# Another list schedule for a chunked attention, and a last row tile finished block by block

## The chip, the cores and the metric

The kernel runs on one core of one Trainium2 chip. The metric is the device time of one execution in microseconds. Every time below that carries a start is counted from the start of the profiled execution's span.

## What is computed

A linear attention with a complex decay feeds a mixture of eight experts, of which each token takes one, and this feeds a plain two-layer network.

```python
B, H, S, D = 4, 8, 768, 48
# attention: per batch and head, over t
S_re, S_im = ar * S_re - ai * S_im + k[t] (x) v[t], ar * S_im + ai * S_re
y[t] = q[t] @ S_re
# experts: x is y as 3072 tokens x 384
e = argmax(x @ w_gate)
x = softmax(x @ w_gate)[e] * sigmoid(x @ w_output_gate)[e] * (relu(x @ w1[e]) @ w2[e])
# second network: 384 -> 2048 -> 384
h = x @ w_in
out = maximum(0.01 * h, h) @ w_out
```

## The kernel before

The sequence is cut into six chunks of 128 positions (`c` from 0 to 5); the four batches form two groups of two (`g`). For each chunk and group an elementwise chain on ScalarE and VectorE makes, from the decay `a`, its logarithm `l` and angle `th`; TensorE sums both over the positions by a product with a triangle (`cum`, 384 columns of moving data, lines 525 and 539); then sine, cosine and the exponentials `ep` and `em` scale q and k into the tiles `qk` (lines 558 and 559).

For each batch and each half of its eight heads there is then a step (`b_step`), 48 in all, with these blocks on TensorE:

- two times four transposes of `qk` into the PSUM tile `tp` (line 603), each copied to `qT` or `kT` by ScalarE or VectorE;
- the scores `sc` (line 612), which VectorE masks into `sT` (line 615);
- the product `yp` of `sT` with v, and from chunk 1 on of `qT` with the state `Z` (lines 624 and 628);
- the state product `kv` (line 639), which VectorE adds to `Z`;
- after the second half four transposes of the result `yT` into `tp` (line 650), copied to `xo`.

After each chunk TensorE makes the logits of the gate (line 583; `lgm`), VectorE routes the tokens (`route`), and POOL scatters the rows `xo` to slots of their expert in `xs_d`. After the last chunk `ranks` orders the experts by size, which the expert layers' loads need.

A TensorE block uses 128, 64 or 32 columns of the array: the rows of the trace write 128\*128, 128\*64 and 128\*32. Transposes, scores and sums use 128, `yp` and `kv` use 64, the gate's logits 32. PSUM tiles rotate: three buffers for `cum`, two for `tp`, one for `sc`.

The order of all this isn't written out by hand. Each piece is recorded as an operation with an engine, a duration in microseconds, the tiles it reads and writes and a priority (`Schedule.op`); `plan` then takes, again and again, the operation that can start first, the one of lower priority number on a tie, and `emit` writes the instructions in that order. Each engine runs its instructions in this order. Priorities are a chunk's base plus an entry of the table `PRIO`.

What follows is written in program order: the expert layers (lines 960 to 962 are the three products of a split into a high and a low part: `hp` the first layer, then the second), and the second network over six row tiles of 512 tokens, `i` from 0 to 5, with 16 slices `f` of its hidden layer each. For a slice TensorE makes nine products into `hp`; ScalarE and VectorE make from it `g`, `gh` and `gl` (lines 1193, 1194, 865 and 868). `second` then multiplies `gh` and `gl` by the slice's weights for four blocks of 128 tokens and adds into the PSUM tiles `yq0` to `yq3`, three matmuls a block. It runs one slice late: the list `late` holds the slice before. After slice 15 each `yq` is scaled into `ot` by ScalarE or VectorE (lines 1177 and 1175) and POOL scatters its rows to the output (line 1178).

Of the kernel before, what the change touches and what calls it, by code (L numbers as in the profile page):

```python
# [20 lines left out]
B, H, S, D = 4, 8, 768, 48  # L21
# [19 lines left out]
NW = NTOK // TW  # L41
# [6 lines left out]

PRIO = {"trig": -14.28, "exp": -4.36, "scaled": 2.94, "next": -3.57, "second": -29.47, "turn": 0.75, "state": 2.81, "rows": 1.73, "gate": -0.63, "route": 12.2}
CUM_BUFS, TP_BUFS, SC_BUFS = 3, 2, 1  # L50
# [48 lines left out]
class Schedule:  # L99
# [14 lines left out]

    def op(self, eng, dur, fn, reads, writes, prio, epoch=None, lat=0.0, gate=None):
        i = len(self.ops)
        deps = set()
        for b in reads:
            deps.update(b.writers)
        for b in writes:  # L120
            deps.update(b.readers)
            deps.update(b.writers)
        new = []
        for b in list(reads) + list(writes):
            r = b.root
            if r.first is None and r.tile is None:
                r.first = i
                new.append(r)
            if i not in r.users:
                r.users.append(i)  # L130
        for b in writes:
            b.writers, b.readers = [i], []
        for b in reads:
            if b not in writes:
                b.readers.append(i)
        deps.discard(i)
        if isinstance(eng, str):
            eng, dur = (eng,), {eng: dur}
        self.ops.append(dict(i=i, uses=[b.root for b in list(reads) + list(writes)], engs=eng, dur=dur, fn=fn, deps=deps, prio=(prio, i), epoch=epoch, new=new, lat=lat, gate=gate))

    def plan(self, table_of, switch=1.28):
# [5 lines left out]
        left = {e: sum(1 for o in ops if o["epoch"] == e) for e in epochs}  # L147
        rings, cur = {}, None

# [3 lines left out]
        def ready(o, eng):  # L153
            t = free.get(eng, 0.0)
            for d in o["deps"]:
                if d not in end:
                    return None
                t = max(t, end[d] + self.LAT.get(by[d], 0.16) + (0.1 if eng == "pe" and by[d] != "pe" else 0.0))
# [7 lines left out]
            for b in o["new"]:  # L166
                ring = rings.setdefault(b.tag, [])
                if len(ring) >= b.bufs:
                    for u in ring[-b.bufs].users:
                        if u not in end:  # L170
                            return None
                        t = max(t, end[u] + 0.2)
            return t

        while todo:
# [13 lines left out]
            i = o["i"]  # L189
            by[i] = eng  # L190
            free[eng] = t + o["dur"][eng]
            end[i] = t + o["dur"][eng] + o["lat"]
            if o["epoch"] is not None:
# [167 lines left out]
def tile_kernel(ctx: ExitStack, tc: tile.TileContext, q, k, v, a_re, a_im, wg, w1, w2, w_in, w_out, cbig, csmall, seq, vseq, wgn, out):  # L361
# [202 lines left out]
    def logits(c, bs, pr):  # L564
# [15 lines left out]
        def lgm():  # L580
            for p2 in range(4):
                for i, b in enumerate(bs):
                    nc.tensor.matmul(out=lp.t[i * 32:(i + 1) * 32], lhsT=WG[:, p2], rhs=yTt[c, b].t[:, p2], start=(p2 == 0), stop=(p2 == 3))
        S.op(PE, 1.2, lgm, [yTt[c, b] for b in bs], [lp], pr)
        ls = S.buf(rt, [P, P], F32, "ls", 2)
# [5 lines left out]
    def b_step(c, b, hh, pr):  # L591
# [28 lines left out]
        def av():  # L620
            for p2 in range(2):
# [3 lines left out]
                if c > 0:  # L625
                    for i in range(2):
                        h = p2 * 2 + i
                        nc.tensor.matmul(out=yp.t[i * 64:i * 64 + 64, hh * 2 + p2], lhsT=Z[:, b, hh * 4 + h], rhs=qT.t[:, h], start=False, stop=True)  # L628
        S.op(PE, 0.51 if c == 0 else 1.04, av, [vt, sT, qT, Zb[b]], [yp], pr)
        if c < NCH - 1:  # L630
# [5 lines left out]
            def kvm():  # L636
                for h in range(4):
                    for i in range(2):
                        nc.tensor.matmul(out=kv.t[i * 64:i * 64 + 64, hh * 4 + h], lhsT=src.t[:, h0 + h, i], rhs=vt.t[:, h0 + h, :D], start=True, stop=True)  # L639
            S.op(PE, 0.61, kvm, [src, vt], [kv], pr + PRIO["state"])  # L640
            if hh == 1:
# [542 lines left out]
    for i in range(NW):  # L1184
        xh, xl = xhl.pop(("b", i))
        for f in range(NF):
# [8 lines left out]
            split(g, hh, hl)  # L1195
            if late:
                second(*late.pop(), range(TT))
# [12 lines left out]
            if f in (9, 11, 13) and i + 1 < NW:  # L1210
                t_split(i + 1, ((f - 9) // 2,))
    second(*late.pop(), range(TT))
    assert done[1] == len(jobs)
# [41 lines left out]
```

## Time and profile before

| what | value |
|---|---|
| median of three runs | 917.2 us (916.55 to 917.49) |
| the profiled execution, its own time | 916.85 us |
| its span in the trace | 915.1 us |
| TensorE busy, share of the span | 881.8 us, 96% |
| VectorE busy | 561.6 us, 61% |
| ScalarE busy | 465.0 us, 51% |
| load of `xe` (672 KB), issue to landing, median | 6.0 us |

The span is what the trace covers; the execution's own time is 1.75 us longer. A TensorE row's busy time runs from the start of its first matmul to the modelled end of its last, and the next block starts before that end; so how long a block takes is read from its start to the start of the next block.

### The profile page before, as it was taken

Reading aid. Unit: us, or ns where it says so; the run is one execution under the profiler, and the core shown is the slowest. Engines: PE = TensorE matmul, PEld = TensorE weight load, DVE = VectorE, ACT = ScalarE, POOL = GpSimd, SP = SyncE. Lnnn points to the kernel's source line nnn. Section 1 sums busy time; section 2 is a strip of 40 time slices with the busy share of each in tenths; the row PEclk is TensorE's granted clock in tenths of the full one; section 3 lists DMA queues with packets and bytes.
Section 4 is the critical chain, followed back from the end, with each engine's and each line's share of the span. In section 5 each row is a group of like instructions: output and inputs, shape, how many; then the busy total and the mean of one; then the engine's idle time right before and its main releaser. Section 6 shows DMA issues by size and latency. Waiting matters only on the chain.

```text
span 915.1 us, 14879 instructions
## 1 busy us (share of the span) xinstructions
PE 881.8 (96%) x5941; PEld 782.0 (85%) x5941; DVE 561.6 (61%) x970; ACT 465.0 (51%) x765; POOL 97.8 (11%) x90
## 2 busy tenths in 40 slices
PE   7888999999979999999999999999999999999996
PEld 3667878887869999999999889999998989899995
DVE  4678999897965767787756533454454454454332
ACT  6898887877633444455555433333343333333232
POOL 5000202101211830000000000100100101001001
PEclk8998999999989999999999999999999999999999
DMA  9834475212345998898867103004004004000001
GB/s 324 355 93 144 163 283 160 81 62 93 131 126 179 207 243 288 272 310 265 271 214 235 43 0 138 36 1 138 36 1 138 35 1 151 22 1 18 19 1 37
DMA packets 56092, 121.58 MB, mean 133 GB/s; under 512 B 8432, under 2 KB 24480, under 8 KB 56016
## 3 DMA queue, kind: packets, MB, share of 16 engines
q1 hardware_dynamic: 49792, 100.87, 34.3%
q0 software_dynamic: 6224, 19.69, 5.8%
q8 instruction: 48, 0.79, 0.4%
q14 instruction: 28, 0.23, 0.1%
HBM read 89.46 MB, written 31.08 MB: 132 GB/s over the span
## 4 chain that ended last, share of the span: by engine, by line
PE 78%; issue 9%; DVE 8%; ACT 3%; DMA 1%; POOL 0%; SPq 0%; POOLq 0%; DVEq 0%; ACTq 0%
PE hp L961 9%; PE hp L960 9%; PE hp L962 9%; PE yq L962 6%; PE yq L960 6%; PE yq L961 6%; PE sc L612 5%; PE tp L603 5%; PE yp L960 3%; PE yp L962 3%; PE yp L961 3%; PE yp L624 3%; PE kv L639 2%; PE cum L525 2%; PE yp L628 2%
## 5 line engine op out<-in xcount | busy, mean ns | idle before, releaser
L960 PE MATMUL hp<-xh,wh 128*128 128x512 f32 (+8 forms) x504 | 186.2, 370 | 1.2 <-DVE hl L1042 1.0
L962 PE MATMUL hp<-xh,wl 128*128 128x512 f32 (+8 forms) x504 | 186.5, 370 | 0.0
L961 PE MATMUL hp<-xl,wh 128*128 128x512 f32 (+8 forms) x504 | 186.4, 370 | 0.1
L1194 DVE TENSOR_TENSOR g<-g,hp 128x512 f32<-128x512 f32 x96 | 65.9, 687 | 156.3 <-ACT g L1193 154.8
L1193 ACT ACTIVATE g<-hp 128x512 f32<-128x512 f32 x96 | 57.4, 597 | 185.2 <-PE hp L962 185.2
L960 PE MATMUL yq<-wh,gh 128*128 128x384 f32 x384 | 129.7, 338 | 0.8 <-ACT gh L865 0.8
L962 PE MATMUL yq<-wh,gl 128*128 128x384 f32 x384 | 129.7, 338 | 0.2
L961 PE MATMUL yq<-wl,gh 128*128 128x384 f32 x384 | 129.0, 336 | 0.0
L868 DVE TENSOR_TENSOR gl<-g,gh 128x512 fp32r<-128x512 f32 x96 | 66.5, 692 | 67.1 <-PE yq L962 39.8
L960 PEld LDWEIGHTS hp<-xh,wh 128*128 128x128 f32 x504 | 95.8, 190 | 12.6 <-DVE hl L1042 3.4
L962 PEld LDWEIGHTS hp<-xh,wl 128*128 128x128 f32 x504 | 95.6, 190 | 12.7
L961 PEld LDWEIGHTS hp<-xl,wh 128*128 128x128 f32 x504 | 95.6, 190 | 9.7 <-DVE xl L868 0.2
L865 ACT ACTIVATE gh<-g 128x512 fp32r<-128x512 f32 x96 | 60.7, 632 | 73.5 <-DVE g L1194 73.5
L1178 POOL DMA_INDIRECT out<-ot,gpair x24 | 24.2, 1009 | 557.7 <-ACT ot L1177 551.8
L868 DVE TENSOR_TENSOR wl<-raw,wh 128x1536 fp32r<-128x1536 f32 x40 | 70.2, 1754 | 20.0 <-ACT wh L865 20.0
L960 PEld LDWEIGHTS yq<-wh,gh 128*128 128x128 f32 x384 | 72.2, 188 | 5.9 <-ACT gh L865 1.6
L961 PEld LDWEIGHTS yq<-wl,gh 128*128 128x128 f32 x384 | 72.3, 188 | 4.3
L962 PEld LDWEIGHTS yq<-wh,gl 128*128 128x128 f32 x384 | 72.0, 188 | 0.9 <-DVE gl L868 0.9
L960 PE MATMUL yp<-hh,wh 128*128 128x448 f32 (+6 forms) x192 | 68.3, 356 | 0.0
L962 PE MATMUL yp<-hh,wl 128*128 128x448 f32 (+6 forms) x192 | 67.1, 350 | 0.0
L961 PE MATMUL yp<-hl,wh 128*128 128x448 f32 (+6 forms) x192 | 67.1, 350 | 0.0
L603 PE MATMUL tp<-CB,qk 128*128 128x128 f32 x384 | 57.5, 289 | 8.3 <-DVE qk L559 4.8
(165 smaller groups left out, 1421.5 us busy)
## 6 DMA issues: line engine op xcount, KB each, us to landing
raw<-w SPq DMA_DIRECT2D x32, 768.0 KB, 6.3
vt<-v SPq DMA_DIRECT2D x12, 512.0 KB, 4.5
raw<-w_in SPq DMA_DIRECT2D x8, 768.0 KB, 8.6
wf<-w SPq DMA_DIRECT2D x16, 384.0 KB, 3.4
raw<-w_out SPq DMA_DIRECT2D x8, 768.0 KB, 6.0
raw<-wf SPq DMA_DIRECT2D x8, 768.0 KB, 5.6
xs_d<-zero POOLq DMA_DIRECT2D x4, 1344.0 KB, 16.4
xe<-xs_d SPq DMA_DIRECT2D x7, 672.0 KB, 6.0
```

Source lines behind the costliest of these rows:

```text
L525: S.op(PE, 0.64, lambda fp=fp, a=a, z=z: nc.tensor.matmul(out=fp.t, lhsT=TRI[c % 2], rhs=th.ap(a, z), start=True, stop=True), [cbb] + th.b ...
L603: nc.tensor.transpose(tp.t[:, h, :], src.t[:, h0 + h].rearrange("p a d -> p (a d)"), IDN)
L612: nc.tensor.matmul(out=sc.t[:, h, :], lhsT=kT.t[:, h], rhs=qT.t[:, h], start=True, stop=True)
L624: nc.tensor.matmul(out=yp.t[i * 64:i * 64 + 64, hh * 2 + p2], lhsT=vt.t[:, h0 + h], rhs=sT.t[:, h], start=True, stop=(c == 0))
L865: nc.scalar.activation(out=hi, in_=src, func=AF.Copy)
L868: nc.vector.tensor_tensor(out=lo, in0=src, in1=hi, op=ALU.subtract)
L960: nc.tensor.matmul(out=out, lhsT=ah, rhs=bh, start=first, stop=False)
L961: nc.tensor.matmul(out=out, lhsT=ah, rhs=bl, start=False, stop=False)
L962: nc.tensor.matmul(out=out, lhsT=al, rhs=bh, start=False, stop=last)
L1178: put = nc.gpsimd.indirect_dma_start(out=rows, out_offset=bass.IndirectOffsetOnAxis(ap=gpair.bitcast(I32)[:, j, 0:1], axis=0), in_=ot, in_ ...
L1193: nc.scalar.activation(out=g, in_=hp, func=AF.Copy, scale=0.01)
L1194: nc.vector.tensor_tensor(out=g, in0=g, in1=hp, op=ALU.max)
```

## The change

The planner is told how many columns of the array an operation uses (`cols`: 128 unless given), and adds 0.1 us (`TURN`) to the start of a TensorE operation whose columns differ from those of the one before. The durations of the narrow operations are set anew, and so is the table of priorities. In the last row tile slices 12 to 15 of the hidden layer are no longer multiplied as they come: `late` keeps them, and after slice 15 the second layer goes block by block, for each block over the four slices.

```diff
-PRIO = {"trig": -14.28, "exp": -4.36, "scaled": 2.94, "next": -3.57, "second": -29.47, "turn": 0.75, "state": 2.81, "rows": 1.73, "gate": -0.63, "route": 12.2}
+PRIO = {"trig": -14.49, "exp": -4.24, "scaled": 2.34, "next": -1.95, "second": -47.41, "turn": -1.83, "state": 19.8, "rows": 2.33, "gate": -35.61, "route": 10.98}
...
+    TURN = 0.1
+
+    def op(self, eng, dur, fn, reads, writes, prio, epoch=None, lat=0.0, gate=None, cols=128):
...
-        rings, cur = {}, None
+        rings, cur, array = {}, None, 128
...
             t = free.get(eng, 0.0)
+            if eng == "pe" and o["cols"] != array:
+                t += self.TURN
...
             free[eng] = t + o["dur"][eng]
+            if eng == "pe":
+                array = o["cols"]
...
-        S.op(PE, 1.2, lgm, [yTt[c, b] for b in bs], [lp], pr)
+        S.op(PE, 1.2, lgm, [yTt[c, b] for b in bs], [lp], pr, cols=32)
...
-        S.op(PE, 0.51 if c == 0 else 1.04, av, [vt, sT, qT, Zb[b]], [yp], pr)
+        S.op(PE, 0.45 if c == 0 else 0.9, av, [vt, sT, qT, Zb[b]], [yp], pr, cols=64)
...
-            S.op(PE, 0.61, kvm, [src, vt], [kv], pr + PRIO["state"])
+            S.op(PE, 0.5, kvm, [src, vt], [kv], pr + PRIO["state"], cols=64)
...
-            if late:
+            if late and not (i == NW - 1 and f > NF - 4):
                 second(*late.pop(), range(TT))
             late.append((i, f, hh, hl))
...
-    second(*late.pop(), range(TT))
+
+    for t in range(TT):
+        for x in late:
+            second(*x, (t,))
```

Each engine keeps its instructions but for about a dozen copies out of PSUM that change between ScalarE and VectorE; what moves is the order. Line numbers of the changed kernel are 6 to 9 higher. Three places show it. The first is TensorE from the logits of chunk 1 on, where the first batches of chunk 2 are worked on. Before:

```order
L583 MATMUL cum<-yT,WG 32x128 x16
L624 MATMUL yp<-sT,vt 64x128 x2
L628 MATMUL yp<-qT,Z 64x128 x2
L624 MATMUL yp<-sT,vt 64x128 x2
L628 MATMUL yp<-qT,Z 64x128 x2
L650 MATMUL tp<-CB,yT 128x128 x4
L612 MATMUL sc<-qT,kT 128x128 x4
L639 MATMUL kv<-vt,qk_108 64x48 x8
L603 MATMUL tp<-CB,qk_107 128x128 x4
L603 MATMUL tp<-CB,qk_108 128x128 x4
L588 MATMUL cum<-CB,ls 128x128
L639 MATMUL kv<-vt,qk_108 64x48 x8
```

And in the changed kernel, from the same logits:

```order
L589 MATMUL cum<-yT,WG 32x128 x16
L630 MATMUL yp<-sT,vt 64x128 x2
L634 MATMUL yp<-qT,Z 64x128 x2
L630 MATMUL yp<-sT,vt 64x128 x2
L634 MATMUL yp<-qT,Z 64x128 x2
L645 MATMUL kv<-vt,qk_108 64x48 x8
L630 MATMUL yp<-sT,vt 64x128 x2
L634 MATMUL yp<-qT,Z 64x128 x2
L630 MATMUL yp<-sT,vt 64x128 x2
L634 MATMUL yp<-qT,Z 64x128 x2
L645 MATMUL kv<-vt,qk_108 64x48 x8
L594 MATMUL cum<-CB,ls 128x128
```

Here the first dimension of the output is the number of columns used. The products `yp` and `kv` of two steps now stand together, and the score block and the transposes that stood among them have moved ahead of the logits or behind the group.

The second place is ScalarE where chunk 1's exponentials are made, just behind its seventh table load; `s` are tiles of the logarithms of chunk 2. Before:

```order
L457 ACTIVATE s_759<-ar 128x768
L541 ACTIVATE ep<-cum 128x384
L457 ACTIVATE s_779<-s_759 128x768
L471 ACTIVATE yT<-yp 128x512
L541 ACTIVATE em<-cum 128x384
L457 ACTIVATE s_795<-ar 128x768
L457 ACTIVATE s_779<-th 128x768
L457 ACTIVATE s_808<-s_795 128x768
L457 ACTIVATE s_779<-s_779 128x768
L471 ACTIVATE xo<-tp 128x384
L471 ACTIVATE qT<-tp 128x512
```

And in the changed kernel:

```order
L463 ACTIVATE s_784<-ar 128x768
L547 ACTIVATE ep<-cum 128x384
L463 ACTIVATE s_791<-s_784 128x768
L547 ACTIVATE em<-cum 128x384
L463 ACTIVATE s_799<-ar 128x768
L463 ACTIVATE s_805<-s_799 128x768
L463 ACTIVATE s_791<-th 128x768
L477 ACTIVATE qT<-tp 128x512
```

The copies `yT` and `xo` of chunk 0 no longer stand ahead of chunk 1's first `qT`; they have moved to the other side of the table load, and one elementwise instruction has moved behind `qT`.

The third place is the end of TensorE's work, the last matmuls into `yq` (with the tiles' numbers: `gh_9079` is slice 15 before). Before:

```order
L960 MATMUL yq2_8670<-wh_6164,gh_9079 128x384
L961 MATMUL yq2_8670<-wl_6165,gh_9079 128x384
L962 MATMUL yq2_8670<-wh_6164,gl_9080 128x384
L960 MATMUL yq3_8674<-wh_6164,gh_9079 128x384
L961 MATMUL yq3_8674<-wl_6165,gh_9079 128x384
L962 MATMUL yq3_8674<-wh_6164,gl_9080 128x384
```

And in the changed kernel, where `gh_8992` to `gh_9055` are slices 12 to 15:

```order
L966 MATMUL yq3_8674<-wh_6164,gh_8992 128x384
L967 MATMUL yq3_8674<-wl_6165,gh_8992 128x384
L968 MATMUL yq3_8674<-wh_6164,gl_8993 128x384
L966 MATMUL yq3_8674<-wh_6164,gh_9021 128x384
L967 MATMUL yq3_8674<-wl_6165,gh_9021 128x384
L968 MATMUL yq3_8674<-wh_6164,gl_9022 128x384
L966 MATMUL yq3_8674<-wh_6164,gh_9038 128x384
L967 MATMUL yq3_8674<-wl_6165,gh_9038 128x384
L968 MATMUL yq3_8674<-wh_6164,gl_9039 128x384
L966 MATMUL yq3_8674<-wh_6164,gh_9055 128x384
L967 MATMUL yq3_8674<-wl_6165,gh_9055 128x384
L968 MATMUL yq3_8674<-wh_6164,gl_9056 128x384
```

The last twelve matmuls all belong to the last block, where before each block had three of them; in return the first-layer products of slice 14 stand 12 matmuls earlier and those of slice 15 stand 24 earlier.

## Rows read from the trace of the kernel before

**Rows 1.** Busy time by engine in stretches; then granted clock, DMA share, GB/s.

```profile
core 0: us, PE busy (x) PEld busy (x) DVE busy (x) ACT busy (x) POOL busy (x), PEclk, DMA share, GB/s
...
30.28:78.74 48.46, 40.99 (x375) 31.47 (x376) 39.41 (x68) 43.54 (x72) 0.00 (x0) 0.93 0.52 184
78.74:84.00 5.26, 5.26 (x49) 4.91 (x52) 3.52 (x6) 3.49 (x7) 0.00 (x0) 0.70 0.58 220
84.00:254.80 170.80, 169.84 (x2022) 140.77 (x2014) 156.27 (x352) 133.44 (x228) 25.57 (x23) 1.00 0.39 134
...
268.64:907.34 638.70, 635.68 (x3336) 588.02 (x3336) 336.56 (x457) 258.19 (x407) 51.61 (x45) 1.00 0.37 118
907.34:915.10 7.76, 0.00 (x0) 0.00 (x0) 0.62 (x1) 0.09 (x1) 3.21 (x4) 0.76 0.31 108
```

**Rows 2.** TensorE's waits, 84 to 254.8: total, times, longest.

```profile
PE sc L612 <- ACT kT L471: 0.6, 1, 0.6
```

**Rows 3.** Timeline of TensorE: start, busy, line, operation, count.

```profile
70.99 0.62 PE L639 MATMUL kv<-vt,qk 128*64 128x48 f32 x16
...
82.71 1.16 PE L612 MATMUL sc<-qT,kT 128*128 128x128 f32 x8
83.80 1.08 PE L583 MATMUL cum<-yT,WG 128*32 128x128 f32 x32
...
107.52 0.67 PE L639 MATMUL kv<-vt,qk 128*64 128x48 f32 x16
108.02 0.40 PE L624 MATMUL yp<-sT,vt 128*64 128x128 f32 x4
...
132.64 1.06 PE L612 MATMUL sc<-qT,kT 128*128 128x128 f32 x8
133.53 1.04 PE L603 MATMUL tp<-CB,qk 128*128 128x128 f32 x8
134.50 0.67 PE L639 MATMUL kv<-vt,qk 128*64 128x48 f32 x16
135.10 0.91 PE L539 MATMUL cum<-l,CB 128*128 128x384 f32 x2
```

**Rows 4.** VectorE: masked scores, 84 to 254.8 (busy, mean, idle before); one timeline row.

```profile
L615 DVE TENSOR_TENSOR sT<-sc,CB 128x512 f32<-128x512 f32 x38 | 26.1, 686 | 8.0 <-PE sc L612 7.2
...
86.28 0.96 DVE L460 TENSOR_TENSOR ep<-ep,qt 128x768 f32<-128x768 f32 x1 [0.18 <-ACT ep L541]
```

**Rows 5.** Timeline of TensorE at the start of chunk 1.

```profile
73.87 0.63 PE L603 MATMUL tp<-CB,qk 128*128 128x128 f32 x4 [1.31 <-DVE qk L559]
76.03 2.92 PE L603 MATMUL tp<-CB,qk 128*128 128x128 f32 x12 [1.53 <-ACT xo L471]
78.73 1.92 PE L612 MATMUL sc<-qT,kT 128*128 128x128 f32 x8
```

**Rows 6.** Timeline where the expert layers begin: a load, and its first use.

```profile
269.85 0.33 SPq L941 DMA_DIRECT2D xe<-xs_d  x1
...
279.00 0.55 PE L955 MATMUL tp<-CB,xe 112*128 112x112 f32 x4
```

**Rows 7.** Timeline of the last row tile, all engines.

```profile
902.31 0.33 PE L960 MATMUL yq<-wh,gh 128*128 128x384 f32 x1
...
904.24 0.34 PE L962 MATMUL yq<-wh,gl 128*128 128x384 f32 x1
904.58 0.69 DVE L868 TENSOR_TENSOR gl<-g,gh 128x512 fp32r<-128x512 f32 x1 [0.70 <-ACT gh L865]
...
905.33 0.44 PE L962 MATMUL yq<-wh,gl 128*128 128x384 f32 x1
...
906.67 0.97 POOL L1178 DMA_INDIRECT out<-ot,gpair  x1 [59.35 <-ACT ot L1177]
...
907.00 0.34 PE L962 MATMUL yq<-wh,gl 128*128 128x384 f32 x1
907.38 0.62 DVE L1175 TENSOR_SCALAR ot<-yq,gpair 128x384 f32<-128x384 f32 x1 [0.42 <-PE yq L962]
...
910.50 0.97 POOL L1178 DMA_INDIRECT out<-ot,gpair  x1 [0.30 <-issue]
```

More of the change, by code (lines that the diff above doesn't have):

```diff
@@ L113, in buf @@
         return Buf(pool, shape, dt, tag, bufs)
-    def op(self, eng, dur, fn, reads, writes, prio, epoch=None, lat=0.0, gate=None):
+    TURN = 0.1
+    def op(self, eng, dur, fn, reads, writes, prio, epoch=None, lat=0.0, gate=None, cols=128):
         i = len(self.ops)
@@ L138, in op @@
             eng, dur = (eng,), {eng: dur}
-        self.ops.append(dict(i=i, uses=[b.root for b in list(reads) + list(writes)], engs=eng, dur=dur, fn=fn, deps=deps, prio=(prio, i), epoch=epoch, new=new, lat=lat, gate=gate))
+        self.ops.append(dict(i=i, uses=[b.root for b in list(reads) + list(writes)], engs=eng, dur=dur, fn=fn, deps=deps, prio=(prio, i), epoch=epoch, new=new, lat=lat, gate=gate, cols=cols))
     def plan(self, table_of, switch=1.28):
```

## The prediction

> **What bounds the kernel now.** I read the stage table of windows first [rows 1]. The program has three parts. In the attention (up to about 264 us) every engine works; from 268.64 to 907.34 TensorE works through the two expert layers with almost no idle time, and the change leaves that stretch alone but for its last row tile; the last 7.8 us hold no TensorE work. So the change acts on the attention and on the end.
>
> Inside the attention the table separates two regimes. From 30.28 to 78.74 TensorE is busy 41.0 of 48.5 us, and the rows show it waiting for the elementwise chain of the next chunk [rows 5]. From 84 to 254.8, which is most of chunks 1 to 5, it is busy 169.84 of 170.80 us at full clock, while VectorE is busy 156.27 and ScalarE 133.44 [rows 1]. The list of waits for that stretch has 0.8 us for TensorE, of which the longer entry is shown [rows 2]. TensorE is the bound there, with VectorE not far behind.
>
> "Busy" does not say that all of this time is needed. Start-to-start times do [rows 3]. A score block (eight matmuls of 128 columns) that stands between 128-column blocks takes 133.53 - 132.64 = 0.89 us. One that stands between two 64- or 32-column blocks takes 83.80 - 82.71 = 1.09. A block of the state product (`kv`, 64 columns) with 128-column work on both sides takes 135.10 - 134.50 = 0.60; one whose follower is also 64 columns wide takes 108.02 - 107.52 = 0.50. Behind another narrow block its busy time is 0.62 (at 70.99) where the others show 0.67, so 0.05 more is lost on entering. None of this shows as waiting.
>
> The Trainium skill, "Trainium Kernel Development and Optimization", Best Practices, says that matmul busy time is a bad measure of distance to the roofline and that the busy share of weight loads is a good one. By it the 140.77 us of PEld in the stretch leave 30 us of room, by the busy row 1 us; the blocks above put the removable part between, and I go by them.
>
> **The change, part by part.** *1. Fewer changes of width.* Same instructions, other order. Counted over the whole order of TensorE up to the first transposes of the expert layers, neighbours of different width fall from 159 to 90; from the first score block of chunk 1 on from 133 to 70. These 63 are 31 excursions from 128 columns to narrow work and back, and one change between narrow widths. An excursion costs 0.20 on a score block that has lost both neighbours plus 0.10 on the narrow block: 0.30 us [rows 3]. The change's own constant, 0.1 us a change, would make it 0.2. 28 of the vanished departures were departures to `kv`, which now stands behind another narrow block and saves the entry's 0.05 as well: 1.4. Sum: 31 x 0.30 + 1.4 = **10.7 us** of TensorE time that would vanish. The changes saved before chunk 1 (159 - 133 = 26 against 90 - 70 = 20) I cost at nothing: TensorE waits for `qk` and for the evacuations there [rows 5]. If those waits were gone, the 6 changes would give 0.9 more.
>
> *2. What becomes of it.* TensorE can pull the end forward only if VectorE follows. Its load is the same, 14.5 us of idle time in the stretch [rows 1], of which 8.0 stand before the masked score copies (`sT`, 38 of them) [rows 4], nearly all while the scores are still being computed. Faster TensorE takes away this idle time and no other. Bounds: 10.7 if the other waits shrink too, 4.0 if only half of the idle time before `sT` can be used, because the copies now queue behind elementwise work. I take **8.0**: this is idle time that is plainly TensorE's fault, and it lies between.
>
> *3. The start of chunk 1.* The first transposes of chunk 1 start at 73.87, stop 1.53 us for an evacuation `xo` at 76.03, and then run at a granted clock below one (0.70 over 78.74 to 84; the first score block is busy 1.92 us where a later one is 1.16) [rows 1, 3, 5]. In the new ScalarE order `xo` has left its place before the first `qT`, and one elementwise instruction has moved behind it; but those copies now stand ahead of the seventh table load and of the exponentials behind it. Between a gain of 1.5 and a loss of 1.5 (the same stop at another place) I take 0.
>
> *4. The routing of the last chunk.* The offsets of its first three batches are now computed behind the last logits, the last batch's behind the whole ranking. Four scatters on POOL's queue and the load of the second half of `xe` on SP's queue follow them. That load is issued at 269.85 and its rows are first transposed at 279.00 [rows 6]: 9.15 us, against some 2.6 us of delay by the moved instructions (an estimate: two more POOL issues at the pitch of part 5) and 6.0 us to landing for a load twice as large (the table above). Hidden; if the cover were gone TensorE would wait there by the excess.
>
> *5. The last row tile.* Before, the second layer of f = 15 finishes its four row blocks in the last 2.4 us, so four evacuations and four scatters bunch: POOL issues start at 906.67 and, in a row, the last at 910.50, while TensorE's last matmul started at 907.00 and the fourth evacuation at 907.38 [rows 7]. Now f = 12 to 15 wait and run block by block. The 24 matmuls of f = 12 and 13 (0.175 us each: 904.24 - 902.31 over eleven) leave the places ahead, so the first layer of f = 15 ends 4.2 us sooner, at 898.1 instead of 902.31. Its `gh` is ready 2.3 us and its `gl` 2.96 us after that (904.58, and 904.58 + 0.69): 901.06. TensorE has only nine matmuls (1.6 us) for block 0 meanwhile, where it had twelve, and waits; its first matmul on `gl` starts at 901.12 (0.06 behind it, as 905.33 is behind 905.27). 36 more follow: the last starts at 901.12 + 36 x 0.175 = 907.42, 0.4 later than now. That is the new wait of this part. But only block 3 is left then: evacuation at 907.80, 0.62 long, issue 0.3 later at 908.72 instead of 910.50. **1.75 us** gained, between 1.2 (another half microsecond of waiting) and 1.8.
>
> Sum against the profiled execution's own time: 916.85 - 8.0 - 1.75 = 907.1. The median of the runs stands 0.35 above that execution, so **907.5 us**.
>
> **The rivals.**
> *A. VectorE takes the bound.* Where TensorE saves, VectorE's masked copy comes late: in the new order 22 score blocks have at most one pair of transposes (0.97 us) between them and the next product with an `sT` (theirs or an older one), where 8 had. For it: VectorE is busy 91% of the stretch [rows 1]. Against it: instructions in a row start sooner than they end, so the share overstates its load. Half of 8.0 is left: 916.85 - 4.0 - 1.75 + 0.35 = 911.5. The Trainium skill, "TensorEngine Tiling (Array Packing)", PSUM Bottleneck, warns that PSUM copies may become the bottleneck once TensorE gets faster; this is that case.
> *B. All of it arrives,* and chunk 1 loses its stop of 1.5: 916.85 - 10.7 - 1.5 - 1.75 + 0.35 = 903.3. For it: TensorE waits almost nowhere today [rows 2].
> *C. Slower.* The order of VectorE is fixed. If `sT` stands behind an elementwise instruction whose input is late, the next product waits. The place is each of the 40 score blocks of chunks 1 to 5. It decides from 12.45 / 40 = 0.31 us a block; at 0.48 (an elementwise instruction over 768 elements, 0.96 us [rows 4], before every second block) the loss is 19.2 and the time 916.85 + 19.2 - 12.45 + 0.35 = 923.9. Against it: today's order, made by the same planner, shows next to no such wait.
> *D. Nothing in the attention.* The elementwise chain sets the pace of each chunk, as at chunk 1 [rows 5], and the saved time turns into waits for `qk`: only the end is gained, 916.85 - 1.75 + 0.35 = 915.5.
>
> **How the numbers follow.** Forecast 0.56 (907.5, own range 905 to 910), A 0.22, B 0.13, C 0.04, D 0.05. A measurement of this kernel can tell about 0.2% (1.8 us) from no change. The range takes in the forecast, most of A and the upper part of B: 903.5 to 912.5. Faster: forecast, A and B, 0.91; same: D, 0.05; slower: C, 0.04.
>
> **What would show it.** Right: from the first score block of chunk 1 to the first transposes of the expert layers the trace shortens by about 8; score blocks of 1.09 become rare and those of 0.89 common; the idle time before `sT` shrinks from 8.0 towards zero; TensorE's waits for `sT`, `qT` and `kT` in the stretch stay below 3 us. In the last tile the last POOL issue starts about 1.3 us behind TensorE's last matmul, instead of 3.5. Wrong: waits for `sT` of 5 us or more (A, C); chunk 1 starting later by more than 2 us (D, or C's cousin at `qk`); the second half of `xe` holding TensorE.

## The result, and the profile after

| | before | after |
|---|---|---|
| median of four runs | 917.35 us (916.55 to 919.05) | 906.88 us (905.19 to 909.38) |
| ratio, 95% interval | | 0.9886 [0.9858, 0.9913] |
| the profiled execution | 916.85 us | 909.38 us, the slowest of the four |

The kernel is 10.5 us faster (8.0 to 13.0), forecast 907.5. Of the steps behind that number, the start of chunk 1 was wrong. Some executions of two kernels below (three of ten of `early_5`, one of six of `split`) are over 1.5% longer at a lower granted clock; medians and ratios leave them out.

Busy time by stretch, columns as in [rows 1]: most of chunks 1 to 5, the expert layers, the end.

```profile
88.30:248.70 160.40, 158.30 (x1987) 137.98 (x1986) 154.27 (x352) 130.54 (x224) 32.01 (x23) 1.00 0.40 141
262.87:901.54 638.67, 635.15 (x3336) 587.56 (x3334) 336.43 (x456) 258.53 (x407) 52.99 (x48) 1.00 0.38 119
901.54:907.60 6.06, 0.00 (x0) 0.00 (x0) 0.62 (x1) 0.00 (x0) 0.97 (x1) 0.78 0.21 73
```

The expert layers are as long as before (638.70 there). In the attention both engines have moved up: TensorE idles 2.1 us of 160.4, VectorE 6.1 (14.5 of 170.8 before). TensorE's waits, which answer to [rows 2], sum to 3.4 us in seven groups (0.8 in two before); the longest three, from 88 to 258 (total, times, longest):

```profile
PE kv L645 <- DVE Z L648: 0.8, 1, 0.8
PE cum L700 <- DVE slot L708: 0.8, 1, 0.8
PE cum L580 <- ACT yT L477: 0.7, 1, 0.7
```

VectorE's masked scores, which answer to [rows 4]; of 8.0 us of idle time before them 3.2 are left:

```profile
L621 DVE TENSOR_TENSOR sT<-sc,CB 128x512 f32<-128x512 f32 x38 | 25.9, 682 | 3.2 <-PE sc L618 2.9
```

TensorE where chunk 1 starts, as in [rows 5], and the first transposes of the expert layers (in the trace before these start at 264.26):

```profile
77.80 1.94 PE L609 MATMUL tp<-CB,qk 128*128 128x128 f32 x8 [7.37 <-DVE qk L565]
...
83.11 1.06 PE L618 MATMUL sc<-qT,kT 128*128 128x128 f32 x8
84.00 1.04 PE L609 MATMUL tp<-CB,qk 128*128 128x128 f32 x8
84.95 1.16 PE L618 MATMUL sc<-qT,kT 128*128 128x128 f32 x8
...
258.30 1.04 PE L961 MATMUL tp<-CB,xe 112*128 112x112 f32 x4
```

From the first score block of chunk 1 (78.73 before) to those transposes the trace takes 175.19 us instead of 185.53: 10.34 less. But that block itself starts 4.38 later. The sum for the two profiled executions: -10.34 + 4.38 - 1.4 at the end (below) - 0.1 between transposes and the first matmul of the first layer = -7.5, as their times differ (916.85 - 909.38).

The last row tile, as in [rows 7]:

```profile
894.12 0.44 PE L966 MATMUL yq<-wh,gh 128*128 128x384 f32 x1 [0.54 <-ACT gh L871]
...
901.20 0.34 PE L968 MATMUL yq<-wh,gl 128*128 128x384 f32 x1
...
901.57 0.62 DVE L1181 TENSOR_SCALAR ot<-yq,gpair 128x384 f32<-128x384 f32 x1 [3.55 <-PE yq L968]
902.47 0.97 POOL L1184 DMA_INDIRECT out<-ot,gpair  x1 [1.15 <-DVE ot L1181]
```

POOL's last issue stands 1.27 behind TensorE's last matmul (3.50 before). Against the first matmul of the expert layers (268.96 before, 262.87 after) that last matmul is 0.28 later, with the 0.54 of waiting for `gh` that step 5 named; from POOL's last issue to the end of the span it takes 5.1 instead of 4.6. Together 0.28 - 2.23 + 0.53 = -1.4.

### The profile page after: what moved, and what is told of

Its sections match the earlier page's. It is cut to its first block, busy times and chain, and to the rows that moved or that the text cites. A ratio compares the mean times of both kernels' runs of the same rounds, so it can differ in the third digit from the quotient of the medians.

```text
span 907.6 us, 14896 instructions
## 1 busy us (share of the span) xinstructions
PE 873.3 (96%) x5941; PEld 782.9 (86%) x5941; DVE 558.1 (61%) x970; ACT 464.6 (51%) x765; POOL 102.7 (11%) x90
## 4 chain that ended last, share of the span: by engine, by line
PE 82%; DVE 10%; ACT 4%; issue 3%; DMA 1%; SPq 0%; POOL 0%; POOLq 0%; DVEq 0%; ACTq 0%
PE hp L967 10%; PE hp L966 10%; PE hp L968 10%; PE yq L968 7%; PE yq L966 7%; PE yq L967 7%; PE sc L618 4%; PE tp L609 4%; PE yp L966 3%; PE yp L968 3%; PE yp L967 3%; PE yp L630 2%; PE kv L645 2%; PE cum L531 2%; PE yp L634 1%
```

## The experiments

Each was timed in alternation with the kernel before, whose median lies between 917.0 and 919.9 us on the chips used; so kernels are compared by their ratios to it. Below, *stretch* is the time from chunk 1's first score block to the first transposes of the expert layers (185.5 before, 175.2 after). *Stream* is an estimate of what TensorE would need for it without any wait: every block at the shortest start-to-start time it has in the trace before, by the widths of its neighbours (179.3 and 167.7). *Waits* is the difference: what is left over, which also holds gaps too short for the profile's list of waits and time at a lower granted clock (1.5 us in the kernel before).

### The two parts alone

`tile_only` is the last two hunks of the change in the kernel before; `sched_only` is the changed kernel with these two hunks undone.

> The kernel before with the edit of the last row tile alone; schedule, durations and priorities of the attention stay as they were. Theory (my step 5): the last POOL issue follows TensorE's last matmul by 1.3 us instead of 3.5, TensorE ends 0.4 later, the end of the program moves by -1.75: 917.35 - 1.75 = 915.6. Rival (read from the trace after): the last scatter takes longer from issue to landing there (3.64 us against 3.07), and this belongs to the new order: then the end moves by -1.2 to -1.4, 916.0 to 916.15. Second rival: the four bunched scatters were hidden behind each other's landing, nothing is gained: 917.3.

> The changed kernel with the old last row tile, so the new order of the attention alone. If the two parts of the change simply add up, its time is that of the changed kernel plus what the tile edit is worth: 906.9 + 1.4 to 1.75 = 908.3 to 908.6, a ratio to the kernel before of 0.990. In the trace the first score block of chunk 1 stands near 83.0 and the first transposes of the expert layers near 258.2, as in the changed kernel. Rival: the shorter attention is partly paid back later (weights that arrive no sooner, a lower granted clock in the expert layers): then it lies above 909.5.

Measured: 0.9982 [0.9968, 0.9997], or -1.65 us (0.3 to 2.9), and 0.9909 [0.9892, 0.9925], -8.3 us. Their product is 0.9891, the changed kernel 0.9886: the parts add up. The gain of the tile is there, and so is the first rival (a slower landing): over all runs of this study the end of the span lies 4.7 to 5.3 behind the last issue with the new tile (ten traces, mean 5.0) and 4.4 to 4.6 with the old one (four, 4.55).

### Where chunk 1 starts

Three runs: the changed kernel again (`after_again`), one with an old priority in chunk 0, and one in which the planner leaves out the price of one table load when it chooses what comes next.

```diff
# c0_turn
-            S.op(PE, 0.43, tr, [src], [tp], pr + PRIO["turn"])
-            evac(t, tp, 512, pr + PRIO["turn"])
+            S.op(PE, 0.43, tr, [src], [tp], pr + (PRIO["turn"] if c else 0.75))
+            evac(t, tp, 512, pr + (PRIO["turn"] if c else 0.75))
# early_5
-                    key = (t, o["prio"], n)
+                    key = (t - (switch if o["epoch"] in (5,) and table_of(o["epoch"]) != cur else 0.0), o["prio"], n)
```

> The changed kernel, with one priority (that of the qT and kT transposes and their evacuations) put back to its old 0.75 in chunk 0 alone. From the middle of chunk 1 on the instruction order of every engine is the one of the changed kernel (70 changes of width from chunk 1's first score on); in chunk 0, ScalarE's sixth table load has 11 copies of qT, kT, yT and xo ahead of it instead of 18 (13 in the kernel before). Theory: the changed kernel's chunk 1 starts 4.3 us late because these copies stand ahead of the table load; here the load starts near 54, the first score block of chunk 1 near 79.5, and 3.0 to 4.3 of the changed kernel's time go: 902.6 to 903.9. Rival 1: the start of chunk 1 is late because the elementwise chain behind the table load (VectorE) is the limit whatever ScalarE does: under 1 us gained, 906 to 907. Rival 2: chunk 1 starts earlier but what it gains is waited for again inside chunks 1 and 2 (TensorE's waits for sT, qT, kT grow by as much): the first transposes of the expert layers stay at 258, time 906 to 907.

> The changed kernel once more, unaltered, as the measure for the other three on the same chip: 905 to 909; from chunk 1's first score block to the expert layers' first transposes 179.8 us (first to first matmul), as in its first trace.

> The changed kernel, with the planner's price of 1.28 for ScalarE's sixth table load (chunk 1's rotary tables) left out of the choice of what comes next. Theory, formed after the run that put back chunk 0's priority: chunk 1 starts when ScalarE's sixth AND seventh table loads are both done early; each is late when copies of chunk 0 that still wait for TensorE stand ahead of it (before: loads at 54.1 and 66.6, first score block of chunk 1 at 78.7; changed kernel 58.5, 71.0, 83.0; chunk 0's old priority 53.1, 72.8, 84.8). In the order made here the sixth load has 13 copies of chunk 0 ahead of it instead of 18, and the seventh only 7 more, the last of them an xo two instructions ahead of the last tables, so that it can stand near 67.5. From the first blocks of chunk 1 on the orders are those of the changed kernel. Then the first score block of chunk 1 stands at 79 to 80 and the whole is 2.8 to 3.5 us faster than the changed kernel: 903.4 to 904.1. Rival 1: TensorE has done less of chunk 0 by then (14 of its blocks instead of 16 products and row transposes), and what it owes makes up for it: gain under 1, 906 to 907. Rival 2: VectorE, at over 90% in chunks 1 to 4, cannot start early what TensorE now can, and TensorE waits for sT or qk in chunk 1: gain under 1 as well, with waits in 84 to 120 above 3 us.

`c0_turn` measured 911.84 us, 0.9941 [0.9925, 0.9958]: slower than the changed kernel, and the theory fell as it was put. Its sixth table load is early, as intended (53.05), but its first score block stands at 84.83. ScalarE's rows show where the time went (start, busy):

```profile
64.74 0.84 ACT L463 ACTIVATE w<-w 128x768 f32<-128x768 f32 x1
66.26 0.49 ACT L477 ACTIVATE xo<-tp 128x384 f32<-128x384 f32 x1 [0.68 <-PE tp L656]
...
70.96 0.60 ACT L477 ACTIVATE yT<-yp 128x512 f32<-128x512 f32 x1 [1.01 <-PE yp L630]
72.30 0.49 ACT L477 ACTIVATE xo<-tp 128x384 f32<-128x384 f32 x1 [0.74 <-PE tp L656]
72.81 1.28 ACT L904 ACT_TABLE_LOAD   x1
```

The elementwise work of the sixth table ends at 65.6; six copies of chunk 0, five of them waiting for TensorE, then hold the seventh load until 72.81. ScalarE's queue is in order, so the exponentials of chunk 1 wait for chunk 0's leftovers. The table loads six and seven in the kernel before, and then in the changed one:

```profile
54.11 1.28 ACT L898 ACT_TABLE_LOAD   x1
...
66.59 1.28 ACT L898 ACT_TABLE_LOAD   x1
```

```profile
58.45 1.28 ACT L904 ACT_TABLE_LOAD   x1
...
70.97 1.28 ACT L904 ACT_TABLE_LOAD   x1
```

In both the seventh follows the sixth by 12.5 us and the first score block follows the seventh by 12.1 (12.0 in `c0_turn`): the 4.3 us by which the sixth load is late come out at the score block undiminished. So each of the two loads can hold chunk 1 back. The Trainium skill, "ScalarE: Activation LUTs", What ACT_TABLE_LOAD costs, states about 1283 ns for the load, which is the 1.28 of these rows; what the load cost here is its place in the queue.

`early_5` then has both loads early (50.63 and 66.32), and its TensorE rows show the start of chunk 1, earlier than the 79 to 80 expected:

```profile
73.15 1.06 PE L609 MATMUL tp<-CB,qk 128*128 128x128 f32 x8 [2.44 <-ACT s L463]
...
76.88 1.16 PE L618 MATMUL sc<-qT,kT 128*128 128x128 f32 x8
```

That is 4.4 earlier than in `after_again` (81.28), and the granted clock shows it as well (1.00 is the higher of its two levels, 2.4 GHz, 0.50 the lower, 1.2 GHz, and figures between are a mean over time); the stretch 74 to 80 in the changed kernel, and in `early_5`:

```profile
74.00:80.00 6.00, 2.20 (x14) 1.90 (x16) 6.00 (x11) 5.51 (x9) 0.00 (x0) 0.63 0.75 254
```

```profile
74.00:80.00 6.00, 5.14 (x43) 4.04 (x42) 6.00 (x11) 4.60 (x8) 0.00 (x0) 1.00 0.41 157
```

In the changed kernel TensorE has stood idle for 7.4 us before 77.80, and eight transposes there are busy 1.94 us where they take 1.04 at full clock. But of the 4.4 us only 2.4 arrive at the expert layers: the stream behind the mark grew by 1.5 (products of chunk 0 that are now owed) and the waits by 0.5. So the expectation was right on the place, and the first rival on half of what it is worth. The whole: 908.58 us, 0.9905 [0.9874, 0.9936] (the quotient of the medians alone would be 0.988), beside `after_again` with 909.31, 0.9883 [0.9869, 0.9898]; the profiled executions are 907.70 and 909.87. The mechanism is shown in the trace, a gain in the timed runs is not; no version here is shown to beat the changed kernel.

### What a change of width costs

The two runs are mirror images and leave the plan alone. After planning, single `kv` blocks are moved in TensorE's order; every other engine's order is the same to the instruction.

```diff
-        for x in self.plan(table_of):
+        for x in self.apart(self.plan(table_of)):      # split, in the changed kernel
+        for x in self.together(self.plan(table_of)):   # join, in the kernel before
...
+    # apart, for a kv block n behind a narrow block, ahead of a 128-column block:
+                    order.insert(pe[2], order.pop(pe[1]))
...
+    # together, for a kv block alone between 128-column blocks, p, up to the next narrow one:
+                        order.insert(last, order.pop(p))
```

> The changed kernel, with 14 blocks of the state product (kv, 64 columns) in chunks 1 to 4, which stand right behind another narrow block, moved behind the one 128-column block that follows: TensorE's order alone, the other engines' orders are the same to the instruction; 28 more changes of width (98 instead of 70 from chunk 1's first score block on). Theory (the price read from the trace: 0.20 on the 128-column block, 0.10 on the narrow one, 0.05 on entering the moved block): 14 x 0.30 to 0.35 = 4.2 to 4.9 us more from chunk 1's first score block to the expert layers (179.8 + 4.2 to 4.9 = 184.0 to 184.7), and as much in the whole: 911.1 to 911.8. Rival: what shortened the attention was the order in which the engines hand work to each other, and a change of width costs nothing by itself or is hidden behind VectorE: under 1.5 us more.

> The kernel before, plan and last row tile as they were; after planning, 13 blocks of the state product (kv) of chunks 1 to 5 that stand alone between 128-column blocks are moved up to three blocks later, next to the following narrow block. TensorE's order alone changes, the other engines' orders are the same to the instruction: 107 changes of width from chunk 1's first score block on instead of 133. It is the mirror of the run that moved 14 such blocks apart in the changed kernel. Theory (0.30 us for an excursion, 0.35 where the moved block's entry is saved as well, and TensorE is the bound from chunk 1 on): from chunk 1's first score block to the expert layers' first transposes 185.5 - 13 x 0.30 to 0.35 = 181.0 to 181.6, and the whole 3.9 to 4.6 less than the kernel before. Rival (the other engines' orders are fixed and set the pace, so fewer changes alone give nothing without a new plan): under 1.5 us.

`split` measured 915.70 us, 0.9955 [0.9941, 0.9970], 6.4 us above `after_again`, more than the 4.2 to 4.9 expected; its stretch is 180.1, 4.9 longer than in the first trace of the changed kernel and 3.1 longer than in the second. (The 179.8 of the expectations of `after_again`, `split` and `turn_00` runs on to the first matmul of the first layer, 262.87 - 83.11; counted like that `split` has 268.24 - 83.53 = 184.7.) One place shows the price without any of that scatter. The changed kernel (product, `kv`, eight transposes, sums), and then `split` (product, four transposes, `kv`, four transposes, sums):

```profile
187.24 0.39 PE L634 MATMUL yp<-qT,Z 128*64 128x128 f32 x4
187.46 0.62 PE L645 MATMUL kv<-vt,qk 128*64 128x48 f32 x16
188.01 1.09 PE L609 MATMUL tp<-CB,qk 128*128 128x128 f32 x8
188.94 0.81 PE L545 MATMUL cum<-l,CB 128*128 128x384 f32 x2
```

```profile
191.59 0.39 PE L661 MATMUL yp<-qT,Z 128*64 128x128 f32 x4
191.90 0.66 PE L636 MATMUL tp<-CB,qk 128*128 128x128 f32 x4
192.49 0.67 PE L672 MATMUL kv<-vt,qk 128*64 128x48 f32 x16
193.09 0.65 PE L636 MATMUL tp<-CB,qk 128*128 128x128 f32 x4
193.59 0.81 PE L572 MATMUL cum<-l,CB 128*128 128x384 f32 x2
```

The same matmuls take 188.94 - 187.24 = 1.70 in the one and 193.59 - 191.59 = 2.00 in the other: 0.30 us for one excursion. From 92 us on, 16 of the 17 `kv` blocks of `split` between 128-column blocks take 0.60, and all but one of the 15 of the changed kernel behind a narrow block 0.55. The rival fell.

`join` measured 916.02 us, 0.9980 [0.9971, 0.9990]: 1.8 us (0.9 to 2.7) for 13 excursions fewer, where the theory wanted 3.9 to 4.6; the rival, under 1.5, is not excluded. Its stretch is 184.6, the stream 3.9 less than before and the waits 2.9 more. One place shows how the gain is lost:

```profile
186.85 0.67 PE L669 MATMUL kv<-vt,qk 128*64 128x48 f32 x16
188.19 0.67 PE L669 MATMUL kv<-vt,qk 128*64 128x48 f32 x16 [0.66 <-DVE Z L672]
188.79 1.16 PE L642 MATMUL sc<-qT,kT 128*128 128x128 f32 x8
```

Two `kv` blocks now stand together, and the second waits for VectorE to have read the first; before, other work stood between them. So a narrow block that stands alone costs its 0.30, but taking it away pays in full only if the other engines' orders fit.

### What the plan needs

Four kernels that differ from the changed one or the one before in a constant or the table: `turn_03` and `turn_00` have `TURN = 0.3` and `TURN = 0.0` in the changed kernel, `old_table` has the old `PRIO` in the changed kernel, `new_table` the new `PRIO` in the kernel before.

> The changed kernel with one constant altered: the planner adds 0.3 us to a block of another width instead of 0.1, which is what the trace charges for an excursion. The order it makes has 82 changes of width up to the first transposes of the expert layers (90 in the changed kernel, 159 before) and 68 from chunk 1's first score on (70, 133); ScalarE's sixth table load has 12 copies ahead of it (18 in the changed kernel, 13 before). Theory (width changes, and the late start of chunk 1 from the copies ahead of the table load): the count is worth 0.3 us, the earlier start of chunk 1 another 3.0 to 4.3, so 902.3 to 903.6. Rival (the planned order is worse in some other way, since work that would be ready is held back for the width): VectorE and ScalarE deliver late, TensorE's waits from 88 us to the end of the attention exceed 6 us instead of 3.4, and the time is 906 or more.

> The changed kernel with the planner's 0.1 us for a change of width set to 0; its new durations and priorities are kept. The order has 116 changes of width from chunk 1's first score block on (70 in the changed kernel, 133 before). Theory: 46 more changes, 23 excursions of 0.30 to 0.35 us, so from chunk 1's first score block to the expert layers 186.7 to 187.9 instead of 179.8; chunk 1 starts earlier (three copies fewer in all ahead of ScalarE's seventh table load), by 1 to 3: the whole 911 to 913. Rival: durations and priorities made the gain, the count of changes is a by-product: 180 to 182 for the same stretch, the whole 904 to 907.

> The kernel before with the new table of priorities alone: its planner does not count changes of width and has its old durations (0.51/1.04 and 0.61); old last row tile. The order has 129 changes of width from chunk 1's first score block on (before 133, changed kernel 70, without the count but with the new durations 116). It asks why the run without the count was slow: TensorE's stream there is 176.5 us at unit prices, yet the stretch to the expert layers took 202.2, so 25.7 us of waits against 6.2 before. Theory (the planner's clock): the new durations hold no cost of a change, so a plan that doesn't count changes runs ahead of the chip by some 0.15 us for each of them and hands VectorE and ScalarE orders for moments that don't come; with the old durations, which hold it on the mean, the waits stay at 5 to 9: stretch 184 to 188, the whole 915 to 919. Rival (the new table only fits the counted plan): waits of 15 and more: 194 or more, the whole 925 or more.

> The changed kernel with the old table of priorities: the planner counts changes and has the new durations. 84 changes of width from chunk 1's first score block on (70 in the changed kernel), TensorE's stream 167.7 + 14 x 0.15 to 0.175 = 169.9 to 170.2; in chunk 0 its order is that of the run with chunk 0's old priority, so chunk 1 starts 1.7 us later than in the changed kernel. Theory (counting is what matters, the table is fine tuning): waits of 7 to 10, stretch 177 to 180, the whole 3.5 to 6 above the changed kernel: 911 to 914. Rival (table and count only work together): waits of 15 and more, 918 or more.

| kernel | ratio, 95% interval | changes of width | stream | stretch | waits |
|---|---|---|---|---|---|
| before | 1 | 133 | 179.3 | 185.5 | 6.2 |
| changed | 0.9886 [0.9858, 0.9913] | 70 | 167.7 | 175.2 | 7.5 |
| changed, again | 0.9883 [0.9869, 0.9898] | 70 | 167.7 | 176.9 | 9.2 |
| `turn_03` | 0.9970 [0.9957, 0.9983] | 55 | 165.8 | 182.4 | 16.6 |
| `turn_00` | 1.0176 [1.0160, 1.0192] | 116 | 176.5 | 202.2 | 25.7 |
| `new_table` | 1.0095 [1.0081, 1.0110] | 129 | 177.7 | 197.5 | 19.8 |
| `old_table` | 1.0201 [1.0188, 1.0214] | 84 | 170.4 | 201.3 | 30.9 |

The 55 of `turn_03` are counted in its trace (67 up to the first transposes of the expert layers); its expectation had 68 and 82. So the kernel with the fewest changes and the shortest stream is not the fastest. My theory failed in all four, each time by the waits; in three of them the rival named beforehand came. The stream follows the changes, as the theory says. The stretch does not: the waits range from 6 to 31 us and decide. My theory of `turn_00`, that new durations without the count let the plan run ahead of the chip, explains at most 25.7 - 19.8 = 5.9, since `new_table` has the old durations and waits nearly as much. In `old_table` the largest group has one place (TensorE's waits from 84 to 262, then the timeline of POOL and ScalarE):

```profile
PE tp L609 <- ACT xo L477: 9.8, 4, 6.8
```

```profile
124.34 4.56 POOL L718 DMA_INDIRECT xs_d<-xo,dest  x1 [109.98 <-ACT s L463]
...
130.51 0.49 ACT L477 ACTIVATE xo<-tp 128x384 f32<-128x384 f32 x1 [4.31 <-DMA xs_d<-xo,dest]
```

Chunk 0's first scatter is issued at 124.34; in the changed kernel its row is

```profile
107.73 1.28 POOL L718 DMA_INDIRECT xs_d<-xo,dest  x1 [93.37 <-ACT em L547]
```

The six buffers of `xo` are full until chunk 0 is scattered, a copy `xo` of chunk 1 waits 4.31 us for a buffer on ScalarE's queue, and TensorE waits behind it for its transposes' tile. In `turn_00`, `new_table` and `turn_03` the waits are spread (no group above 3.3 us in the attention), and why these orders wait more stays open.

### Is VectorE the next bound?

`z_short` alters one line of the changed kernel, of which this part differs:

```diff
-out=Z[:, b, :, :D], in0=kv.t, scalar=4.0, in1=Z[:, b, :, :D]
+out=Z[:, b, :, :4], in0=kv.t[:, :, :4], scalar=4.0, in1=Z[:, b, :, :4]
```

> The changed kernel; the 20 updates of the state (Z, VectorE, 128x384, 0.47 us from start to start) are done on 4 of each 48 columns only, so the kernel leaves out eleven twelfths of the state update. Every engine's order is the one of the changed kernel. From the traces so far: between chunk 1's first score block and the expert layers' first transposes the changed kernel takes 175.2 to 176.9 us, of which 167.7 is its TensorE stream at traced unit prices; 7.0 to 8.7 are waits, 4.3 to 6.2 of them in chunks 1 to 3, while VectorE's busy share there is 95 to 99%. Theory (VectorE has become the second bound in chunks 1 to 3): about 0.35 x 16 = 5.6 us of VectorE's work in chunks 1 to 4 goes, and the stretch shortens by 2.5 to 5, to about 171 to 173. Rival (what TensorE waits for there is the hand-over through ScalarE and the buffers, not VectorE's load): under 1 us, 174.5 or more.

Measured: 913.41 us, 0.9931 [0.9916, 0.9946], a stretch of 179.7: slower than the changed kernel with less to do. From 120 to 228 VectorE (the third time) is busy 100.2 of 108 us instead of 106.5, and TensorE (the first) gains nothing; first `z_short`, then the changed kernel:

```profile
120.00:228.00 108.00, 105.16 (x1330) 91.51 (x1330) 100.23 (x233) 88.68 (x153) 13.43 (x12) 1.00 0.36 132
```

```profile
120.00:228.00 108.00, 107.45 (x1376) 94.42 (x1377) 106.52 (x239) 90.04 (x157) 17.70 (x12) 1.00 0.39 140
```

TensorE loses 4.5 us in three places (at 111, 145 and 183) in which the profile shows nothing that it waits for ("issue"); the largest:

```profile
183.36 0.26 PE L645 MATMUL kv<-vt,qk 128*64 128x48 f32 x3
183.78 0.33 PE L645 MATMUL kv<-vt,qk 128*64 128x48 f32 x4 [0.15 <-issue]
184.50 0.32 PE L645 MATMUL kv<-vt,qk 128*64 128x48 f32 x4 [0.39 <-issue]
185.91 0.35 PE L645 MATMUL kv<-vt,qk 128*64 128x48 f32 x5 [1.09 <-issue]
```

Without them the stretch would be as long as in the changed kernel. But its first blocks run at a granted clock of 0.50 (from 80 to 82), where those of the changed kernel have 1.00:

```profile
80.21 1.92 PE L618 MATMUL sc<-qT,kT 128*128 128x128 f32 x8
...
83.24 1.06 PE L618 MATMUL sc<-qT,kT 128*128 128x128 f32 x8
```

From one score block to the next this is 3.03 us where the changed kernel takes 84.95 - 83.11 = 1.84. Without the pauses and these 1.2 us the stretch would be 174.0, 1.2 less than in the first trace of the changed kernel: between the rival (under 1) and the theory (2.5 to 5). So VectorE's load as the bound got little support, and how much it holds back stays open.

## Why the prediction was right, and where it was wrong

*Step 1, 10.7 us of TensorE time in 31 excursions of 0.30.* Right. `split` shows 0.30 by itself, and block by block the stream falls by 179.3 - 167.7 = 11.6, of which 1.2 are two `kv` blocks of 0.60 [rows 3] that the new order has ahead of the mark, the first score block of chunk 1: 10.4. As foreseen, score blocks of 0.89 became common: 27 of the 36 from 92 us on, where 10 were.

*Step 2, 8.0 of it arrive.* Right in size. The two profiled executions give 10.3, but traces of one order differ: 185.5 and 184.3 (`tile_only`) for the old one, 175.2, 176.9, 175.0 (`sched_only`) and 175.1 (`c0_turn`) for the new one, which is 9.4 between the means. Two parts of this only moved to the other side of the mark. One is the 1.2 of the two `kv` blocks. The other is the clock: in the old order TensorE, which had stopped for 1.53 us just before, still runs at a granted clock of 0.50 (from 78 to 80) behind the mark, where the new one is back at 1.00. The blocks behind the first score block (78.73 in [rows 5]), in the kernel before:

```profile
80.44 1.73 PE L603 MATMUL tp<-CB,qk 128*128 128x128 f32 x8
82.11 0.67 PE L639 MATMUL kv<-vt,qk 128*64 128x48 f32 x16
```

and in `tile_only`, from that score block:

```profile
79.14 1.33 PE L612 MATMUL sc<-qT,kT 128*128 128x128 f32 x8
...
81.28 0.67 PE L639 MATMUL kv<-vt,qk 128*64 128x48 f32 x16
```

The score block and eight transposes take 82.11 - 78.73 = 3.38 and 81.28 - 79.14 = 2.14, against 0.89 + 0.97 = 1.86 later [rows 3]: 1.5 and 0.3, whose difference is the one between the two old traces. With both parts out, 9.4 - 1.2 - 0.9 = 7.3 arrive. `split` agrees: it puts 14 of the 31 excursions back with every other engine's order fixed and loses 3.1 to 4.9, where 14 of 31 parts of 8.0 are 3.6. The reason given was too narrow. VectorE's idle time shrank by 8.4, but before `sT` only by 4.8; "this idle time and no other" does not hold.

*Step 3, the start of chunk 1 at 0, between -1.5 and 1.5.* This step failed: +4.4 between the profiled executions, and 2.1 to 4.4 over the traces of the two orders (78.73 and 79.14 before, 81.28, 82.17 and 83.11 after). I priced the place at which TensorE had stopped [rows 5] and named the copies that moved ahead of the seventh table load, but did not follow the chain one load further up. The sixth load had slid behind five more copies of chunk 0 (18 instead of 13), and its delay came out whole at the score block. A start later by more than 2 us was named as a sign of being wrong, for rival D; it came, D did not. What the miss cost is less than 4.4: in the profiled pair 1.2 + 1.5 = 2.7 of it is the time that step 2 has just given back, and `early_5` moved the start 4.4 ahead, of which 2.4 arrived.

*Step 4, the routing hidden.* Right. The second half of `xe` is issued at 265.70 and first transposed at 272.81, 7.1 us later where [rows 6] have 9.15; TensorE does not wait for it.

*Step 5, -1.75 at the end.* Right in mechanism, a little large. POOL's last issue is 1.27 behind the last matmul in all ten traces with the new tile and 3.5 in the four without: -2.23, as forecast. But from the first layer's first matmul TensorE's last one is later by 0.9 on the mean (639.1 against 638.2) where I had 0.4, and the landing 0.45 slower: -0.9 in the traces, -1.65 (0.3 to 2.9) in the timed runs.

*The sum* was -8.0 + 0 - 1.75 = -9.75; measured are -10.5 and, in `after_again`, 0.9883 of 919.57 or -10.8. Between the profiled executions it was only -7.5: +4.4 missed in step 3, 2.3 more than 8.0 in step 2, 0.35 less in step 5. The first two are mostly one thing: without the 2.7 us that moved across the mark they are +1.7 and 0.4 less than 8.0. The other 2.5 to 3 us are the distance of the execution profiled after the change from its own median (909.38 and 906.88, against 916.85 and 917.35 before), and what made it the slowest stays open. So the traces account for 7.5 of the 10.5 us, and that the timed runs met the forecast although step 3 was missed is partly luck.

*The rivals.* A (VectorE) did not come: most of the stream's gain arrived, and `z_short` gave the bound little support. B's price of 10.7 looks nearer in the profiled pair, but only until the 2.7 us across the mark are taken out; its other condition, the lost stop at chunk 1, came out reversed. C got 0.04 on the argument that "today's order, made by the same planner, shows next to no such wait". `turn_00`, `new_table` and `old_table` show that this argument is worth little: the same planner, with one constant or the table changed, made orders that wait 20 to 31 us, slower than the kernel before by 1.0 to 2.0%. The forecast side was right, its certainty was not earned.

## What to carry to other kernels

Price a change of layout by start-to-start times with and without the neighbour, not by busy shares: 0.30 us per excursion was invisible in 169.84 of 170.80 us busy. When a plan moves work, follow the chain that starts a stage back through every table load of its in-order queue, and count what now stands ahead of each. A planner that is told one more cost makes another order altogether: what it saves can be counted beforehand, what it waits cannot be inferred from the old order, so candidate orders have to be run, and a term that helps on paper (`turn_03`) can lose.

## What was not expected of the hardware

TensorE paused inside a block whose operands were all there: 16 matmuls of `kv` took 2.83 us in `z_short` (183.36 to 186.19) where the same block took 0.55 in the changed kernel, and 1.27 when that kernel ran again. The stretch around the pause, first in `z_short` and then in the changed kernel (the last figure but one is the busy share of the 16 DMA engines):

```profile
183.00:186.50 3.50, 1.86 (x29) 1.59 (x26) 1.49 (x4) 0.70 (x2) 1.83 (x2) 1.00 1.03 407
```

```profile
183.00:186.50 3.50, 3.50 (x60) 3.31 (x56) 3.50 (x7) 3.04 (x5) 2.98 (x2) 1.00 0.95 337
```

Both times four scatters and the loads of the next chunk fill the DMA engines; only once TensorE pauses. The Trainium skill, "Runtime: NRT & Kernel Launch", Instruction fetch mechanics, says that engines refill their instructions in 16 KiB blocks through a DMA queue of their own, mostly hidden. The traces agree on the size (48 packets, 0.79 MB), but show no packet of that queue between 183 and 186.5, so what TensorE waited for stays open. Such pauses are part of why traces of one order differ, by up to 1.9 us in the stretch: in the repeated changed kernel two of them, at 150 and 184, make 1.05 of the 1.74 us by which it is longer than the first trace. Between the two traces of the old order it was the clock.
